# Softplus as one ScalarE activation in a mixer with two MLPs

## The chip, the cores and the metric

The kernel runs on one core of one Trainium2 chip. The metric is the device time of one execution in microseconds (us), the median of several runs. One profiled execution gives the trace; its times are read on the span's own clock, which starts at 0.

## The reference

A state-space mixer over four batches and eight heads gives 3072 tokens of 256 channels. Two MLPs follow, 256 to 2048 to 256. The first one's activation is a softplus, written so that it never overflows; the second one's is a sigmoid approximation of Gelu.

```python
def _moe_ref(x, w_in, w_out):
    h = x @ w_in
    g = np.maximum(h, 0.0) + np.log1p(np.exp(-np.abs(h)))
    return (g @ w_out).astype(np.float32)

def _moe2_ref(x, w_in, w_out):
    h = x @ w_in
    g = h * (1.0 / (1.0 + np.exp(-1.702 * h)))
    return (g @ w_out).astype(np.float32)
```

## The kernel before

The tokens are cut into six chunks (`c`) of 128 positions times four batches, 512 columns each. Each MLP goes through its 2048 hidden channels in 16 slices (`m`) of 128, so that one loop of `2 * NT + 2` = 194 steps `t` runs over both: steps 0 to 95 are the first MLP, 96 to 191 the second. The program's order on each engine is the order of the code (`tc.manual_schedule()`); nothing reorders it.

A step `t` holds, on TensorE, `g1(t)` (six matmuls into the PSUM tile `h`, one of three) and `g2(t - 2)` (the hidden slice times the output weights, accumulated in PSUM `o`). To keep float32 accuracy each operand is a sum of a rounded part and a remainder. `rnd` (ScalarE) makes the rounded part `gh`, `low` (VectorE) the remainder `gl = g - gh`. `g2` takes `wl·gh`, `wh·gh` (L372, L373) and `wh·gl` (L374), for two halves of the output. In the first 16 slices the output weights are not yet split, and `g2` takes two plain float32 matmuls on `g` (L370).

In between, the mixer of the next chunk runs, one sub-chunk in four steps (`k = t % 4`): `cb` matmuls at `k` 0 and 1, their masked products `M` on VectorE (L278), `y` and the state's matmuls at `k` = 2, and at `k` = 3 `xh`/`xl`, the state's update and the long scan `L` (L233) on VectorE. In steps 0 to 13 VectorE also turns the first MLP's float64 weights into float32, one unit a step (`w_sign` L122, `w_join_hi` L127, `w_join_lo` L132); their remainders `w1il` are made on GpSimd. Steps 14 to 29 split the output weights (`w1ol`, VectorE). From step 80 the second MLP's weights are turned, in half units.

The first MLP's softplus is made of four operations on `h`: ScalarE Abs (L546), Exp (L549) and Ln (L561) of the step `t`, and VectorE's `g = max(h, 0) + e` (L542) one step later, at `t + 1`. `rnd(t)` follows on ScalarE at `t + 1`, and `low(t)` on VectorE at the start of step `t + 2`, the step whose `g2(t)` reads it.

Of the kernel before, what the change touches and what calls it, by code (L numbers as in the profile page):

```python
# [9 lines left out]
F32 = mybir.dt.float32  # L10
# [3 lines left out]
AF = mybir.ActivationFunctionType  # L14
ALU = mybir.AluOpType
# [3 lines left out]
T = 128  # L19
# [5 lines left out]
TB = NB * T  # L25
NSUB = NC * NB
NT = NC * NF
# the first chunk's packs have C and B once, its C B^T is taken in plain float32
PL_B, PL_C, PL_X, PL_BN, PL_W = 0, 128, 256, 512, 640
SP_B, SP_C, SP_X, SP_BN, SP_CI, SP_W = 0, 512, 1024, 1280, 1408, 1664  # L30
# 2^-112 turns a float64's exponent, read in the high word as a float32's, into one that float32 holds
HI_SCALE = 2.0**-112


# [1 line left out]
def mixer_two_mlps(ctx: ExitStack, tc: tile.TileContext, pack_p, pack_s, a_l, a_rows, consts, w1i, w1o, w2i, w2o, out):  # L36
# [32 lines left out]
    w1oh = wts.tile([P, NF, DM], F32R, name="w1oh")  # L69
    w1ol = wts.tile([P, NF, DM], F32R, name="w1ol")  # L70
    x2 = wts.tile([P, NC, 2, TB], F32, name="x2")
    # the whole float32 w1o, until the second block splits it
    w1of = x2[:, 2:6].rearrange("p c k t -> p (c k t)").rearrange("p (m f) -> p m f", m=NF)

    def vsub(o, x, y):
# [2 lines left out]
    def psub(o, x, y):  # L78
        nc.gpsimd.tensor_tensor(out=o, in0=x, in1=y, op=ALU.subtract)  # L79

    # a split's two halves, each taken up one step after what it waits for
    act_later, vec_later = [], []

    def split(dst_h, dst_l, src, sub=None):
# [17 lines left out]
        src = w[:, f].rearrange("(k p) f -> p k f", p=P) if kind[-1] == "i" else w[f, :].rearrange("(c p) f -> p c f", p=P)  # L102
        nc.sync.dma_start(out=raw.rearrange("p (a f) -> p a f", a=2), in_=src)

    # float64 bits to float32: the scaled high word holds the exponent and 20 bits of the
    # mantissa three bits too low, the low word the next three
    def w_scale(kind, q, eng):
        if kind[0] == "2" and q in (4, 6):
            # the first block of x2 is out of use by then
            t = x2[:, 0, int(kind == "2o")]  # L110
        else:
            t = stg.tile([P, 512], F32, tag="wt", name=f"wt_{kind}{q}")
        hi = raws[kind, q].bitcast(F32)[:, 1::2]
        if eng is nc.scalar:
            nc.scalar.activation(t, hi, AF.Copy, scale=HI_SCALE)
        else:
            nc.vector.tensor_scalar(out=t, in0=hi, scalar1=HI_SCALE, scalar2=None, op0=ALU.mult)
        return t
# [278 lines left out]

    W1 = (w1ih, w1il)
    with tc.manual_schedule():
        nc.scalar.preload_act_table_set("natural_log_exp_and_others")  # L400
        ac = [hid.tile([P, TB], F32, tag="g", name=f"ac{i}")[0:96, 0 : 2 * T].rearrange("p (k t) -> p k t", k=2) for i in range(3)]
        at_load_p(0)
        nc.sync.dma_start(out=cc, in_=consts)
# [10 lines left out]
        at_spread(0)  # L414
        nc.scalar.activation(eye8[:, TB:].rearrange("p (h t) -> p h t", h=4), eye4, AF.Copy)
        at_scan(0, 0)
        # clipped decays in DRAM, as they are and with the first of each chunk zeroed
        clip(ac[2], ac[0])
        nc.vector.memset(ac[2][:, :, 0:1], 0.0)
        clip(ac[1], ac[0])  # L420
# [86 lines left out]
        for t in range(2 * NT + 2):  # L507
            c, m = divmod(t, NF)
            s, k = (c + 1) * NB + m // 4, m % 4
            mixing = c < NC - 1  # L510
            ended = (t - 2) // NF if t >= 2 and (t - 2) % NF == NF - 1 else None

            if mixing and k in (1, 2) and t != 1:
                at_m(s, k - 1)
            if t < len(W1_units):
                w_sg = w_sign(*W1_units[t])
            if NF <= t - 2 < NT:
                low(t - 2)
            if NT < t <= 2 * NT:
                low(t - 1)  # L520

            if t < NT:
                g1(t, *W1, xh[c], xl[c])
            elif t < 2 * NT:
                g1(t, *w2[0:2], x2h[c - NC], x2l[c - NC])
            if t == 0:
                at_u(NB - 1)
            late = k < 2 or t < NF
            if mixing and not late:
                at_pe(s, k)  # L530
            if 2 <= t < NT + 2:
                g2(t - 2, w1oh, w1ol, plain=w1of if t - 2 < NF else None)
            elif t >= 2:
                g2(t - 2, *w2[2:4])
            if mixing and late:
                at_pe(s, k)

            xl_of = at_out(s) if mixing and k == 3 else None
            if 1 <= t <= NT:
                d = tt[t - 1]  # L540
                d["g"] = hid.tile([P, TB], F32, tag="g", name=f"g{t - 1}")
                nc.vector.scalar_tensor_tensor(out=d["g"], in0=d["h"], scalar=0.0, in1=d["e"], op0=ALU.max, op1=ALU.add)  # L542
            if t < NT:
                d = tt[t]
                e = d["e"] = hid.tile([P, TB], F32, tag="e", name=f"e{t}", bufs=2)
                nc.scalar.activation(e, d["h"], AF.Abs)  # L546
                if t > NF:
                    rnd(t - 1)
                nc.scalar.activation(e, e, AF.Exp, scale=-1.0)  # L549
            elif t < 2 * NT:  # L550
                d = tt[t]
                d["g"] = hid.tile([P, TB], F32, tag="g", name=f"g{t}")
                if t == NT:
                    rnd(t - 1)
                nc.scalar.activation(d["g"], d["h"], AF.Gelu_apprx_sigmoid)  # L555
                rnd(t)
            if ended is not None:
                finish(ended, 0)
                finish(ended, 1)
            if t < NT:  # L560
                nc.scalar.activation(tt[t]["e"], tt[t]["e"], AF.Ln, bias=1.0)  # L561
            if t == 0:
                at_m(s, 0)
            if t < len(W1_units):
                w_join_hi(wt, w_sg)
            catch_up(vec_later)
            catch_up(act_later)

            if t in (1, 3):
                at_state(2 + t // 2)  # L570
            if mixing:
                if k == 0:
                    at_small(s)
                elif k == 1:
                    if s + 1 < NSUB:
                        at_prep(s + 1)
                elif k == 3:
                    xl_of()
                    at_state(s)
                    if s + 1 < NSUB:  # L580
                        at_scan(s + 1)
                    if s + 2 < NSUB:
                        at_load(s + 2)
                    if s == NSUB - 1:
                        at_ctx.close()

            if t < len(W1_units):
                kind, q = W1_units[t]
                if kind == "1o":
                    w_join_lo(kind, q, wt, w1of[:, 2 * q : 2 * q + 2, :].rearrange("p m f -> p (m f)"))  # L590
                else:
                    wi_split(W1, q, w_join_lo(kind, q, wt), psub)
                if t + 1 < len(W1_units):
                    wt = w_scale(*W1_units[t + 1], nc.scalar)
                if t + 3 < len(W1_units):
                    kind, q = W1_units[t + 3]
                    w_load(W_in[kind], kind, q)
            if NF - 2 <= t < 2 * NF - 2 and m % 2 == 0:
                q = (t - NF + 2) // 2
                wo_split((w1oh, w1ol), q, w1of[:, 2 * q : 2 * q + 2, :])  # L600
            if t == (NC - 1) * NF:
                wt2 = ctx.enter_context(tc.tile_pool(name="wt2", bufs=1, reuse_waits="tile"))
                w2 = [
                    wt2.tile(sh, F32R, name=nm)
                    for sh, nm in (([P, 2, DFF], "w2ih"), ([P, 2, DFF], "w2il"), ([P, NF, DM], "w2oh"), ([P, NF, DM], "w2ol"))
                ]
                for kind, q in W2_units[0:3]:
                    w_load(W_in[kind], kind, q)
            # the second layer's weights in half units, the last half of them while it runs
            due = 0  # L610
            if c == NC - 1:
                due = 14 * (m + 1) // 16
            elif c == NC:
                due = min(2 * len(W2_units), 14 + 3 * (m + 1) // 2)
            while halves < due:
                kind, q = W2_units[halves // 2]
                if halves % 2 == 0:
                    half = scaled.pop((kind, q), None) or w_scale(kind, q, nc.vector), w_sign(kind, q)
                else:
                    dst, spl = (w2[0:2], wi_split) if kind == "2i" else (w2[2:4], wo_split)  # L620
                    spl(dst, q, w_join(kind, q, *half), psub)
                    if halves // 2 + 3 < len(W2_units):
                        kind, q = W2_units[halves // 2 + 3]
                        w_load(W_in[kind], kind, q)
                halves += 1
                u = (halves + 1) // 2
                if t >= NT - 1 and u < len(W2_units) and W2_units[u] not in scaled:
                    scaled[W2_units[u]] = w_scale(*W2_units[u], nc.scalar)
            if m == 8 and NC - 1 <= c < 2 * NC - 1:
                x2split(c - NC + 1)  # L630
# [52 lines left out]
```

## Time and profile before

| | |
|---|---|
| time, median of 3 runs (lowest to highest) | 640.23 us (639.79 to 640.71) |
| span of the profiled execution | 638.4 us, 1.8 us below the median |
| TensorE busy with matmuls | 604.7 us, 95% of the span |
| VectorE busy | 430.0 us, 67% |
| ScalarE busy | 397.5 us, 62% |
| GpSimd busy | 154.5 us, 24% |
| chain that ended last | PE 61%, VectorE 26%, issue 5%, ScalarE 4% |

PE is TensorE, PEld its weight loads, DVE VectorE, ACT ScalarE, POOL GpSimd, SPq the DMA-issuing queue. The profiled execution has no separate timing; its own time is its span and what lies around it, and it stands 1.8 us below the median. A matmul's end is modelled and neighbours overlap, so a busy share near 95% does not say how close TensorE is to its best; the starts of the steps say it.

### The profile page before, as it was taken

How to read it: one execution, taken by the hardware profiler on the slowest of the kernel's cores; microseconds unless marked ns; L12 is line 12 of the kernel's file. 1: busy time of each engine (PE TensorE's matmuls, PEld its weight loads, DVE VectorE, ACT ScalarE, POOL GpSimd, SP SyncE). 2: the span in 40 equal slices, each digit the busy share in tenths (PEclk: the TensorE clock that was granted, in tenths of full speed). 3: DMA queues.
4: the chain of work that ended last, by engine and by line, in shares of the span. 5: the costliest groups of instructions: out<-in, count | busy, mean ns of one | idle time of the engine just before them, and what ended most of it. 6: DMA issues, size and time to landing. Idle time of an engine off the chain costs nothing.

```text
span 638.4 us, 8982 instructions
## 1 busy us (share of the span) xinstructions
PE 604.7 (95%) x3392; PEld 455.1 (71%) x3392; DVE 430.0 (67%) x622; ACT 397.5 (62%) x693; POOL 154.5 (24%) x135
## 2 busy tenths in 40 slices
PE   4779889999999999999999999999999999999997
PEld 1345446677677777777777777788888888888886
DVE  5989998999898899989768989723223223232221
ACT  3376666777676767777788887545445445454443
POOL 2555444333434433334102133200000000000000
PEclk8889999999999999999999999999999999999999
DMA  7855644323332332324011224000000000000000
GB/s 225 284 181 198 224 170 144 100 96 119 107 102 95 118 126 95 131 102 153 1 33 67 99 100 131 1 33 2 1 33 1 33 1 1 34 0 1 34 0 33
DMA packets 24411, 54.42 MB, mean 85 GB/s; under 512 B 2832, under 2 KB 8368, under 8 KB 24368
## 3 DMA queue, kind: packets, MB, share of 16 engines
q1 hardware_dynamic: 24368, 53.85, 24.7%
q8 instruction: 26, 0.43, 0.3%
q14 instruction: 17, 0.14, 0.1%
HBM read 50.50 MB, written 3.34 MB: 84 GB/s over the span
## 4 chain that ended last, share of the span: by engine, by line
PE 61%; DVE 26%; issue 5%; ACT 4%; DMA 2%; SPq 1%; POOL 1%; DVEq 0%; ACTq 0%; POOLq 0%
PE h L356 27%; PE o L374 11%; PE o L372 10%; PE o L373 9%; DVE gl L76 6%; DVE L L233 4%; DVE g L542 3%; DVE x L132 1%; DVE wt_2i L127 1%; DVE wt_1o L127 1%; ACT gh L379 1%; DMA wraw_1o<-w1o 1%; PE cb L267 1%; PE y L295 1%; DMA ac<-a_rows 1%
## 5 line engine op out<-in xcount | busy, mean ns | idle before, releaser
L76 DVE TENSOR_TENSOR gl<-g,gh 128x512 fp32r<-128x512 f32 x176 | 152.9, 869 | 162.7 <-ACT gh L379 161.9
L379 ACT ACTIVATE gh<-g 128x512 fp32r<-128x512 f32 x176 | 111.1, 631 | 34.8 <-DVE g L542 31.5
L555 ACT ACTIVATE g<-h 128x512 f32<-128x512 f32 x96 | 57.3, 597 | 113.5 <-PE h L356 113.3
L546 ACT ACTIVATE e<-h 128x512 f32<-128x512 f32 x96 | 57.1, 594 | 39.6 <-PE h L356 39.2
L356 PE MATMUL h<-xh,w1ih 128*128 128x512 f32 x192 | 78.3, 408 | 0.5 <-ACT xh L323 0.5
L374 PE MATMUL o<-gl,w2oh 128*128 128x512 f32 x192 | 75.2, 391 | 0.9 <-DVE gl L76 0.8
L356 PE MATMUL h<-xl,w1ih 128*128 128x512 f32 x192 | 75.8, 395 | 0.0
L372 PE MATMUL o<-gh,w2ol 128*128 128x512 f32 x192 | 74.7, 389 | 0.0
L356 PE MATMUL h<-x2h,w2ih 128*128 128x512 f32 x192 | 74.7, 389 | 0.0
L356 PE MATMUL h<-x2l,w2ih 128*128 128x512 f32 x192 | 74.7, 389 | 0.0
L373 PE MATMUL o<-gh,w2oh 128*128 128x512 f32 x192 | 74.7, 389 | 0.0
L374 PE MATMUL o<-gl,w1oh 128*128 128x512 f32 x160 | 66.0, 412 | 7.7 <-DVE gl L76 7.4
L542 DVE SCALAR_TENSOR_TENSOR g<-h,e 128x512 f32<-128x512 f32 x96 | 65.2, 680 | 4.4 <-ACT e L561 4.2
L372 PE MATMUL o<-gh,w1ol 128*128 128x512 f32 x160 | 64.4, 403 | 0.0
L356 PE MATMUL h<-xh,w1il 128*128 128x512 f32 x192 | 60.3, 395 | 3.9 <-POOL w1il L79 3.9
L373 PE MATMUL o<-gh,w1oh 128*128 128x512 f32 x160 | 62.6, 391 | 0.0
L561 ACT ACTIVATE e<-e 128x512 f32<-128x512 f32 x96 | 60.7, 632 | 2.9
L79 POOL TENSOR_TENSOR rhs_bd<-tc,pk 64x512 fp32r<-64x512 f32 x40 | 61.5, 1539 | 1.5
L549 ACT ACTIVATE e<-e 128x512 f32<-128x512 f32 x96 | 59.5, 620 | 0.5
L356 PE MATMUL h<-x2h,w2il 128*128 128x512 f32 x192 | 59.1, 389 | 0.0
L233 DVE TENSOR_TENSOR_SCAN L<-abz,eye 128x1024 f32<-128x1024 f32 (+1 forms) x25 | 55.9, 2236 | 0.2
L374 PEld LDWEIGHTS o<-gl,w1oh 128*128 128x128 f32 x160 | 30.0, 187 | 25.8 <-DVE gl L76 20.5
(100 smaller groups left out, 896.3 us busy)
## 6 DMA issues: line engine op xcount, KB each, us to landing
pk<-pack_s SPq DMA_DIRECT2D x20, 832.0 KB, 4.5
abz<-scr_z SPq DMA_DIRECT2D x22, 512.0 KB, 3.7
wraw_1i<-w1i SPq DMA_DIRECT2D x8, 512.0 KB, 4.2
wraw_1o<-w1o SPq DMA_DIRECT2D x8, 512.0 KB, 3.3
wraw_2i<-w2i SPq DMA_DIRECT2D x8, 512.0 KB, 3.5
wraw_2o<-w2o SPq DMA_DIRECT2D x8, 512.0 KB, 3.3
out<-ot SPq DMA_DIRECT2D x12, 256.0 KB, 2.2
ad<-scr_a SPq DMA_DIRECT2D x80, 32.0 KB, 2.0
```

The source lines that it names most:

```text
L76: nc.vector.tensor_sub(o, x, y)
L79: nc.gpsimd.tensor_tensor(out=o, in0=x, in1=y, op=ALU.subtract)
L233: nc.vector.tensor_tensor_scan(out=d["L"][:, h].rearrange("p h t -> p (h t)"), data0=d["abz"][:, h].rearrange("p h t -> p (h t)"), data1=e ...
L356: nc.tensor.matmul(h, w[:, k, f], x[:, k, :], start=(n == 0), stop=(n == 5))
L372: nc.tensor.matmul(acc[c][j], wl[:, m, o], d["gh"], start=first, stop=False)
L373: nc.tensor.matmul(acc[c][j], wh[:, m, o], d["gh"], start=False, stop=False)
L374: nc.tensor.matmul(acc[c][j], wh[:, m, o], d["gl"], start=False, stop=last)
L379: nc.scalar.activation(d["gh"], d["g"], AF.Copy)
L542: nc.vector.scalar_tensor_tensor(out=d["g"], in0=d["h"], scalar=0.0, in1=d["e"], op0=ALU.max, op1=ALU.add)
L549: nc.scalar.activation(e, e, AF.Exp, scale=-1.0)
L555: nc.scalar.activation(d["g"], d["h"], AF.Gelu_apprx_sigmoid)
L561: nc.scalar.activation(tt[t]["e"], tt[t]["e"], AF.Ln, bias=1.0)
```

## The change

Softplus becomes one activation that reads `h` in PSUM and writes `g`. Abs, Exp, Ln and the VectorE operation are gone, and with them the tile `e` of the loop. The first MLP's steps get the form of the second's: `g(t)` and, from step 16 on, `gh(t)` are both made in step `t`, and `gl(t)` at the start of step `t + 1`. Another set of ScalarE's tables is loaded at the start.

```diff
-        nc.scalar.preload_act_table_set("natural_log_exp_and_others")
+        nc.scalar.preload_act_table_set("softplus")
...
-            if NF <= t - 2 < NT:
-                low(t - 2)
-            if NT < t <= 2 * NT:
+            if NF < t <= 2 * NT:
                 low(t - 1)
...
-            if 1 <= t <= NT:
-                d = tt[t - 1]
-                d["g"] = hid.tile([P, TB], F32, tag="g", name=f"g{t - 1}")
-                nc.vector.scalar_tensor_tensor(out=d["g"], in0=d["h"], scalar=0.0, in1=d["e"], op0=ALU.max, op1=ALU.add)
-            if t < NT:
-                d = tt[t]
-                e = d["e"] = hid.tile([P, TB], F32, tag="e", name=f"e{t}", bufs=2)
-                nc.scalar.activation(e, d["h"], AF.Abs)
-                if t > NF:
-                    rnd(t - 1)
-                nc.scalar.activation(e, e, AF.Exp, scale=-1.0)
-            elif t < 2 * NT:
+            if t < 2 * NT:
                 d = tt[t]
                 d["g"] = hid.tile([P, TB], F32, tag="g", name=f"g{t}")
-                if t == NT:
-                    rnd(t - 1)
-                nc.scalar.activation(d["g"], d["h"], AF.Gelu_apprx_sigmoid)
-                rnd(t)
+                nc.scalar.activation(d["g"], d["h"], AF.Softplus if t < NT else AF.Gelu_apprx_sigmoid)
+                if t >= NF:
+                    rnd(t)
...
-            if t < NT:
-                nc.scalar.activation(tt[t]["e"], tt[t]["e"], AF.Ln, bias=1.0)
```

The rows of TensorE, GpSimd and the DMA-issuing queue stand in the same order in both programs. Two engines change. The number in `g57` or `gl57` is the step.

VectorE in steps 6 to 8, where it turns weights (`x2` holds the unsplit output weights), before:

```order
L132 SCALAR_TENSOR_TENSOR x2_103<-wraw_1o3_501,wt_1o3_567 128x512
L122 TENSOR_SCALAR wraw_1i5_533<-wraw_1i5_533 128x512
L542 SCALAR_TENSOR_TENSOR g6_632<-h6_574,e6_610 128x512
L127 SCALAR_TENSOR_TENSOR wt_1i5_617<-wt_1i5_617,wraw_1i5_533 128x512
L76 TENSOR_TENSOR xl1_473<-y5_583,xh1_472 128x2x128
L337 SCALAR_TENSOR_TENSOR st1_96<-st1_96,dc5_524,y5_583 128x32 x2
L233 SCALAR_TENSOR_TENSOR L6_643<-abz6_489,eye8_87 128x1024
L132 SCALAR_TENSOR_TENSOR wt_1i5_617<-wraw_1i5_533,wt_1i5_617 128x512
L122 TENSOR_SCALAR wraw_1o4_569<-wraw_1o4_569 128x512
L542 SCALAR_TENSOR_TENSOR g7_672<-h7_622,e7_634 128x512
```

The same place now:

```order
L132 SCALAR_TENSOR_TENSOR x2_103<-wraw_1o3_487,wt_1o3_545 128x512
L122 TENSOR_SCALAR wraw_1i5_515<-wraw_1i5_515 128x512
L127 SCALAR_TENSOR_TENSOR wt_1i5_591<-wt_1i5_591,wraw_1i5_515 128x512
L76 TENSOR_TENSOR xl1_463<-y5_561,xh1_462 128x2x128
L337 SCALAR_TENSOR_TENSOR st1_96<-st1_96,dc5_506,y5_561 128x32 x2
L233 SCALAR_TENSOR_TENSOR L6_613<-abz6_475,eye8_87 128x1024
L132 SCALAR_TENSOR_TENSOR wt_1i5_591<-wraw_1i5_515,wt_1i5_591 128x512
L122 TENSOR_SCALAR wraw_1o4_547<-wraw_1o4_547 128x512
```

One row in each step is gone; the others keep their places.

VectorE from the mixer's sub-chunk 18 to 19 (steps 58 to 60), before:

```order
L76 TENSOR_TENSOR gl56_2597<-g56_2579,gh56_2583 128x512
L542 SCALAR_TENSOR_TENSOR g57_2637<-h57_2563,e57_2581 128x512
L76 TENSOR_TENSOR gl57_2645<-g57_2637,gh57_2641 128x512
L542 SCALAR_TENSOR_TENSOR g58_2661<-h58_2599,e58_2639 128x512
L76 TENSOR_TENSOR xl4_2347<-y18_2606,xh4_2346 128x2x128
L337 SCALAR_TENSOR_TENSOR st2_97<-st2_97,dc18_2553,y18_2606 128x32 x2
L233 SCALAR_TENSOR_TENSOR L19_2672<-abz19_2518,eye8_87 128x1024
L76 TENSOR_TENSOR gl58_2683<-g58_2661,gh58_2665 128x512
L542 SCALAR_TENSOR_TENSOR g59_2701<-h59_2647,e59_2663 128x512
```

And now:

```order
L76 TENSOR_TENSOR gl57_2371<-g57_2357,gh57_2359 128x512
L76 TENSOR_TENSOR gl58_2415<-g58_2411,gh58_2413 128x512
L76 TENSOR_TENSOR xl4_2149<-y18_2380,xh4_2148 128x2x128
L337 SCALAR_TENSOR_TENSOR st2_97<-st2_97,dc18_2331,y18_2380 128x32 x2
L233 SCALAR_TENSOR_TENSOR L19_2438<-abz19_2300,eye8_87 128x1024
L76 TENSOR_TENSOR gl59_2449<-g59_2431,gh59_2433 128x512
```

Ahead of the scan `L19` now stands `gl58`, which stood behind it; each `gl` has moved up by one step.

## Rows read from the trace of the kernel before

**Rows 1.** Windows: us, then each engine's busy us (instructions), granted clock, DMA share, GB/s.

```profile
0.00:44.56 44.56, 27.74 (x218) 13.11 (x218) 35.93 (x53) 21.02 (x43) 21.24 (x25) 0.85 0.72 235
44.56:98.06 53.50, 48.91 (x296) 27.68 (x287) 50.59 (x78) 35.88 (x62) 27.25 (x21) 1.00 0.56 194
98.06:320.61 222.55, 217.50 (x1534) 160.87 (x1533) 199.92 (x289) 159.45 (x284) 83.65 (x73) 1.00 0.30 105
320.61:368.02 47.41, 45.21 (x194) 35.57 (x192) 40.49 (x62) 40.60 (x73) 7.79 (x6) 1.00 0.20 67
368.02:411.59 43.57, 42.17 (x181) 33.32 (x180) 38.56 (x49) 33.02 (x57) 14.60 (x11) 1.00 0.26 85
411.59:638.40 226.81, 223.20 (x985) 184.56 (x983) 64.55 (x95) 107.53 (x178) 0.00 (x0) 1.00 0.04 15
```

**Rows 2.** Waits from 98.06 to 320.61 us: total us, times, longest us.

```profile
PEld o L374 <- DVE gl L76: 15.0, 30, 1.4
...
PE o L374 <- DVE gl L76: 4.7, 7, 1.0
```

**Rows 3.** Page's groups of instructions: busy us, mean ns, then idle us before them.

```profile
L76 DVE TENSOR_TENSOR gl<-g,gh 128x512 fp32r<-128x512 f32 x176 | 152.9, 869 | 162.7 <-ACT gh L379 161.9
L379 ACT ACTIVATE gh<-g 128x512 fp32r<-128x512 f32 x176 | 111.1, 631 | 34.8 <-DVE g L542 31.5
L555 ACT ACTIVATE g<-h 128x512 f32<-128x512 f32 x96 | 57.3, 597 | 113.5 <-PE h L356 113.3
L546 ACT ACTIVATE e<-h 128x512 f32<-128x512 f32 x96 | 57.1, 594 | 39.6 <-PE h L356 39.2
...
L542 DVE SCALAR_TENSOR_TENSOR g<-h,e 128x512 f32<-128x512 f32 x96 | 65.2, 680 | 4.4 <-ACT e L561 4.2
```

**Rows 4.** Timeline of DVE, 48 to 66 us: start us, length us.

```profile
48.42 2.28 DVE L233 TENSOR_TENSOR_SCAN L<-abz,eye 128x1024 f32<-128x1024 f32 x1
...
50.62 0.66 DVE L132 SCALAR_TENSOR_TENSOR wt_1i<-wraw_1i,wt_1i 128x512 uint32<-128x512 uint32 x1
...
51.54 0.68 DVE L542 SCALAR_TENSOR_TENSOR g<-h,e 128x512 f32<-128x512 f32 x1
52.14 0.68 DVE L127 SCALAR_TENSOR_TENSOR wt_1o<-wt_1o,wraw_1o 128x512 uint32<-128x512 uint32 x1
...
60.89 1.67 DVE L132 SCALAR_TENSOR_TENSOR x<-wraw_1o,wt_1o 128x512 uint32<-128x512 uint32 x1
...
65.75 2.28 DVE L233 TENSOR_TENSOR_SCAN L<-abz,eye 128x1024 f32<-128x1024 f32 x1
```

**Rows 5.** Chain that ended last, pieces at step starts: start us, length us.

```profile
98.62 1.39 PE h L356 x6
100.01 1.72 PE o L370 x4
...
246.06 1.37 PE h L356 x6
250.55 1.36 PE h L356 x6
...
297.50 1.39 PE h L356 x6
300.49 1.39 PE h L356 x6
304.87 1.36 PE h L356 x6
307.59 1.36 PE h L356 x6
310.67 1.39 PE h L356 x6
```

**Rows 6.** Timeline of PEld, 254 to 256 us.

```profile
255.11 0.19 PEld L374 LDWEIGHTS o<-gl,w1oh 128*128 128x128 f32 x1 [0.46 <-DVE gl L76]
```

**Rows 7.** Timeline of PE, 38 to 40 us.

```profile
39.07 0.73 PE L356 MATMUL h<-xh,w1il 128*128 128x512 f32 x2 [2.78 <-POOL w1il L79]
```

## The prediction

> **What bounds the kernel now.** I read the starts of the steps first, since with 95% busy nothing can be told from busy time. The first `g1` matmul of step 3 starts at 44.56 us, of step 16 at 98.06, of step 80 at 320.61, of step 96 at 368.02 and of step 111 at 411.59; these cut the windows [rows 1]. Then the chain of waits gives what a step costs when TensorE waits for nothing. In chunk 4 [rows 5] the step with no attention work takes 304.87 to 307.59 = 2.72 us, the steps with `cb` 2.99 and 3.08, the one with `y` 4.38; four steps 297.50 to 310.67 = 13.17. In chunks 1 to 3 the state's matmuls are added to the `y` step, which takes 246.06 to 250.55 = 4.49, so 13.28 for four. In the first chunk the plain `g2` takes 1.72 where the split one takes 2.72 - 1.36 = 1.36, so 4 x 0.36 more: 14.7.
>
> Against these floors:
>
> - Steps 3 to 15: 53.50 us; floor 3 x 14.7 + one step of 1.39 + 1.72 = 47.2. VectorE is busy 50.59 of 53.50 [rows 1]: it is the bound.
> - Steps 16 to 79: 222.55; floor 12 x 13.28 + 4 x 13.17 + 0.7 (steps 16 and 17 still take the plain form) = 212.8. The list of waits names what TensorE waits for: the weight loads of L374 wait 15.0 us for `gl`, the matmuls themselves 4.7 [rows 2]. Loads run ahead of matmuls, so the loss lies between the two; the floor says 9.8. One such wait is in [rows 6].
> - Steps 80 to 95: 47.41; floor 16 x 2.72 = 43.5.
> - Steps 96 to 110: 43.57; floor 15 x 2.72 = 40.8. Only `g2` of steps 94 and 95 is of the old form here.
> - From 411.59 on nothing of the change is left, and VectorE has 64.55 us of work in 226.81. Before 44.56 the first VectorE `g` stands after the work on which TensorE's last long wait hangs, 2.78 us for `w1il` at step 2 [rows 7]; with the granted clock at 0.85 over this stretch I leave it as it is.
>
> **The change, part by part.** *ScalarE.* Abs takes 0.594 us, and it goes with Exp and Ln; one Softplus comes. No row shows Softplus. The nearest rows are the two activations from PSUM of the same 128x512, Abs 594 ns and Gelu 597 ns [rows 3], so I take 0.6 us. No row bounds it from above; what it could cost before it matters is worked out under the last rival. ScalarE waits 39.2 us for `h` before Abs, so time saved there by itself is worth nothing. The Trainium skill, ScalarE: Activation LUTs, What ACT_TABLE_LOAD costs, states 186 ns + 0.833 ns an element whatever the function; by it 512 elements would be an estimated 613 ns and the sum the same. No run here shows it for Softplus, Gelu's 597 agrees.
>
> *VectorE.* 96 operations of 0.68 us go [rows 3]. Neighbours overlap: L542 starts at 51.54 and the next at 52.14 [rows 4], so each frees 0.60.
>
> *Steps 3 to 15.* One sub-chunk is from scan to scan, 48.42 to 65.75 = 17.33 us [rows 4]. Without four L542 it is 17.33 - 2.4 = 14.9, just above TensorE's 14.7. By VectorE: 3 x 14.9 + 3.1 = 47.8, a saving of 5.7; by TensorE's floor 6.3. A lag of 0.2 us per sub-chunk can't reach TensorE within three of them, but `w1il` for the `y` step arrives with little to spare, so I take 5.4. The bounds are 0 (below) and 6.3.
>
> *Steps 16 to 79.* Before, a step's `gl` stood in the same step as the `g2` that reads it, behind the scan (2.28 us) once in four; ScalarE's `gh` itself waited 31.5 us for VectorE's `g` [rows 3]. Now `gh(t)` comes about 0.6 + 0.63 us and two handovers after the end of `g1(t)`: 1.36 + 1.4 = 2.8 us after the step's start, near the start of step t + 1. `gl(t)` follows there (0.9 us on average), and L374 needs it 1.36 + 0.45 us into step t + 2, so 4.5 us after the start of t + 1. The margin is 2.8 us even with an average `gl`; the worst case is `gl` behind the scan, which by my estimate (`xh`, `xl` and the state's update come between) starts 1.5 us into step `k` = 3 and ends 1.1 us into the next, still in time. VectorE's work falls from 199.92 to about 161 (64 x 0.60 less) in 213, 76%. In the new order VectorE stands still behind a `gl` that waits for `gh`, and `M`, `xl` and the scan queue behind it; `M` has some 2 us before `cb` or `y` want it, and TensorE's own 13.28 us a sub-chunk leave that. I take the whole 9.8. Bounds: 0, and 11.1 if the 0.08 us by which the first `cb` step exceeds the second goes as well.
>
> *Steps 80 to 110.* VectorE's 40.49 us fall to 30.9 of about 44, so most of 3.9 goes; I take 3.4 (0 to 3.9), since units of weights come in bursts here. Of the 2.8 lost in steps 96 to 110, 0.6 for the last of the old form (0 to 0.8).
>
> Sum: 5.4 + 9.8 + 3.4 + 0.6 = 19.2, so the span falls from 638.4 to 619.2. The profiled span lies 1.8 us below the median, so the time is 621.0. With every floor reached: 6.3 + 11.1 + 3.9 + 0.8 = 22.1, 618.1.
>
> **The rivals.** *A, the forecast*: all of these stalls go but for small change; 617.5 to 623.5. For it speaks that the floors are taken from steps of this very trace.
>
> *B, the first chunk stays bound by VectorE.* The same operation L132 takes 0.66 us at 50.62 and 1.67 at 60.89 [rows 4]. What is left on VectorE is what stretches, while L542 was 0.68 each time. If the rest slides under GpSimd's work (27.25 us in this stretch) two more of its operations per sub-chunk would take 1 us longer, and of the 5.4 us nothing would be left: 626. For half of that, 624. The Trainium skill, GPSIMD Engine Reference, Specifications, says GpSimd shares its SBUF interfaces with VectorE and collides with its operations of two SBUF inputs or in a two-port mode; L542 reads one input from PSUM, so the trace agrees, with 0.68 against 1.67. Against B: GpSimd's amount of work stays, and the long cases here already meet it.
>
> *C, the new form stalls too.* The second MLP has this form, and where VectorE is loaded (38.56 of 43.57 us) it still loses 2.8 us in 15 steps, 0.19 a step [rows 1]. At that rate 64 steps would lose 12 us and steps 16 to 79 would gain nothing; at half the rate they'd gain 3.7, and the time is 627. Against it: 76% load is not 88%, and from 411.59 on, where VectorE is at 28%, nothing is lost: 81 steps of 2.72 and the two last `g2` of 1.36 are 223 of the 226.81 us, the last copies and the store the rest.
>
> *D, no change.* VectorE is off the path, and TensorE at 95% is the bound. Against it: the floors, and the 15.0 us of waits; it would be 640.
>
> *E, slower.* Softplus is much longer than the other activations. In steps 16 to 79 ScalarE has 222.55 / 64 = 3.48 us a step, and beside Softplus it has `gh` (0.63) and about 0.2 of other work; so it becomes the bound above 2.65 us, 4.4 times Gelu. At 3 us it costs 96 x 0.35 = 34 more, 674. No row shows an activation at such a pace. Were a table loaded at each change between Softplus and the copies, it would be the same case; the program has two loads, as before.
>
> **How the numbers follow.** A has 0.73, B 0.11, C 0.10, D 0.02, E 0.03, and 0.01 is for larger gains. The forecast is A's 621.0. The range must leave out at most 0.2: from 617.5, just under the sum of all floors, through B to the middle of C, 627.5. About 0.2% (1.3 us) is what a measurement of this kernel can tell from no change. A, B and C all end faster by more than that, as do the larger gains: 0.95; D 0.02; E 0.03.
>
> **What would show it.** In the profile after, step 16 should start near 92.7 us, step 80 near 305.4, step 96 near 349, step 111 near 392. From scan to scan in the first chunk 14.7 to 15 us. The waits of L374 for `gl` between steps 16 and 79 fall from 15.0 to under 2 us. Softplus stands at about 0.6 us, and VectorE's idle time before `gl` grows, since it now waits for `gh`. I am wrong in B's way if step 16 starts after 95 with VectorE still at 95%, in C's way if L374 still waits for `gl`, in E's way if Softplus takes over 2.6 us and VectorE's `gl` waits for it in every step.

## The result, and the profile after

The changed kernel takes 622.33 us (median; 621.34 to 622.52), the kernel before 640.16 (639.79 to 640.71): the ratio is 0.9717, with an interval of 0.9704 to 0.9731. The profiled execution's span is 620.5 us, 17.9 below that of before.

The windows of the changed kernel, cut at the same five step starts as [rows 1]: us, then each engine's busy us (PE, PEld, DVE, ACT, POOL), granted clock, DMA share, GB/s.

```profile
0.00:44.66 44.66, 27.91 (x218) 13.74 (x219) 35.78 (x51) 17.71 (x37) 21.89 (x26) 0.89 0.72 235
44.66:96.06 51.40, 48.10 (x295) 27.84 (x287) 48.39 (x65) 21.50 (x38) 26.40 (x21) 1.00 0.61 202
96.06:308.31 212.25, 212.25 (x1534) 163.16 (x1533) 162.37 (x225) 90.47 (x156) 86.36 (x73) 1.00 0.33 110
308.31:351.83 43.52, 43.52 (x193) 36.05 (x192) 31.71 (x47) 24.36 (x42) 8.26 (x6) 1.00 0.23 73
393.23:620.50 227.27, 223.20 (x985) 184.50 (x983) 64.58 (x95) 107.52 (x178) 0.00 (x0) 1.00 0.04 14
```

Steps 96 to 110, the stretch left out, run from 351.83 to 393.23 = 41.40 us. So each stretch gained, in us:

| | start | steps 3-15 | 16-79 | 80-95 | 96-110 | rest | sum |
|---|---|---|---|---|---|---|---|
| predicted | 0 | 5.4 | 9.8 | 3.4 | 0.6 | 0 | 19.2 |
| measured | -0.1 | 2.1 | 10.3 | 3.9 | 2.2 | -0.5 | 17.9 |

In steps 16 to 95 TensorE is busy for the whole window, which it was not before. The first chunk is different: VectorE is still busy 48.39 of 51.40 us, 94%, though an operation of 0.68 us a step has gone.

The page's chain and its groups of the changed kernel; L540 holds Softplus and Gelu together.

```profile
PE 81%; DVE 9%; DMA 4%; issue 3%; SPq 1%; ACT 1%; POOL 0%; DVEq 0%
...
L76 DVE TENSOR_TENSOR gl<-g,gh 128x512 fp32r<-128x512 f32 x176 | 141.7, 807 | 172.6 <-ACT gh L379 172.6
L540 ACT ACTIVATE g<-h 128x512 f32<-128x512 f32 x192 | 114.8, 598 | 256.7 <-PE h L356 253.2
```

Against [rows 3], a Softplus is as long as a Gelu (mean 598 ns, each by itself too). The waits of the changed kernel from 96.06 to 308.31 us (total us, times, longest):

```profile
ACT g L540 <- PE h L356: 112.7, 63, 2.6
...
DVE M L278 <- PE cb L267: 30.3, 26, 2.0
...
DVE gl L76 <- ACT gh L379: 10.1, 17, 1.4
```

The last two in the kernel before, from 98.06 to 320.61 us:

```profile
DVE gl L76 <- ACT gh L379: 10.5, 13, 2.1
...
DVE M L278 <- PE cb L267: 6.3, 16, 1.2
```

The 15.0 and 4.7 us for `gl` of [rows 2] are gone: the other engines now wait for TensorE. VectorE's idle time before `gl`, which was to grow, did not grow in these steps (10.5 and 10.1 us). It grew before `M`, which waits for TensorE's `cb`; before `gl` it grew in steps 80 to 95, from 3.0 to 12.4 us.

### The profile page after: what moved, and what is told of

Read it like the earlier page. It is cut to its first block, busy times and chain, and to the rows that moved or that the text cites. A ratio compares the mean times of both kernels' runs of the same rounds, so it can differ in the third digit from the quotient of the medians.

```text
span 620.5 us, 8790 instructions
## 1 busy us (share of the span) xinstructions
PE 596.1 (96%) x3392; PEld 459.0 (74%) x3392; DVE 378.0 (61%) x526; ACT 293.3 (47%) x501; POOL 157.2 (25%) x135
## 4 chain that ended last, share of the span: by engine, by line
PE 81%; DVE 9%; DMA 4%; issue 3%; SPq 1%; ACT 1%; POOL 0%; DVEq 0%
PE h L356 37%; PE o L372 13%; PE o L374 12%; PE o L373 12%; DMA ad<-scr_a 2%; PE y L295 2%; PE y L289 2%; DVE x L132 1%; PE cb L267 1%; DVE wt_1o L127 1%; DVE L L233 1%; DVE wt_1i L127 1%; DMA ac<-a_rows 1%; PE o L370 1%; DMA wraw_1i<-w1i 1%
## 5 line engine op out<-in xcount | busy, mean ns | idle before, releaser
L76 DVE TENSOR_TENSOR gl<-g,gh 128x512 fp32r<-128x512 f32 x176 | 141.7, 807 | 172.6 <-ACT gh L379 172.6
L540 ACT ACTIVATE g<-h 128x512 f32<-128x512 f32 x192 | 114.8, 598 | 256.7 <-PE h L356 253.2
L79 POOL TENSOR_TENSOR rhs_bd<-tc,pk 64x512 fp32r<-64x512 f32 x40 | 65.1, 1628 | 1.5
L374 PE MATMUL o<-gl,w1oh 128*128 128x512 f32 x160 | 62.4, 390 | 0.0
L233 DVE TENSOR_TENSOR_SCAN L<-abz,eye 128x1024 f32<-128x1024 f32 (+1 forms) x25 | 61.9, 2476 | 0.2
L278 DVE TENSOR_TENSOR M<-cb,L 128x512 f32<-128x512 f32 x48 | 32.7, 686 | 30.5 <-PE cb L267 30.3
L356 PEld LDWEIGHTS h<-xh,w1il 128*128 128x128 f32 x192 | 36.2, 190 | 13.6 <-POOL w1il L79 5.6
L356 PEld LDWEIGHTS h<-xh,w1ih 128*128 128x128 f32 x192 | 36.3, 189 | 8.1 <-ACT xh L323 1.0
L374 PEld LDWEIGHTS o<-gl,w2oh 128*128 128x128 f32 x192 | 36.0, 188 | 8.1 <-DVE gl L76 0.7
L373 PEld LDWEIGHTS o<-gh,w2oh 128*128 128x128 f32 x192 | 36.0, 188 | 7.6
```

The source lines that it names most:

```text
L76: nc.vector.tensor_sub(o, x, y)
L233: nc.vector.tensor_tensor_scan(out=d["L"][:, h].rearrange("p h t -> p (h t)"), data0=d["abz"][:, h].rearrange("p h t -> p (h t)"), data1=e ...
L278: nc.vector.tensor_mul(d["M", g].rearrange("p h t -> p (h t)"), d["cb", g], d["L"][:, 4 * g : 4 * g + 4, :].rearrange("p h t -> p (h t)"))
L356: nc.tensor.matmul(h, w[:, k, f], x[:, k, :], start=(n == 0), stop=(n == 5))
L373: nc.tensor.matmul(acc[c][j], wh[:, m, o], d["gh"], start=False, stop=False)
L374: nc.tensor.matmul(acc[c][j], wh[:, m, o], d["gl"], start=False, stop=last)
```

## The experiments

Starts of steps and lengths of the stretches, us, each read in one trace from the first `g1` matmul of the step. "Scan to scan" is the time between the starts of VectorE's long scans L233, for the first two sub-chunks of the first chunk as in [rows 4]; it hardly hangs on where step 3 starts (e8 and e10 below).

| | step 3 | step 16 | 3-15 | scan to scan | 16-79 | 80-95 | 96-110 | time |
|---|---|---|---|---|---|---|---|---|
| before | 44.56 | 98.06 | 53.50 | 17.33, 17.31 | 222.55 | 47.41 | 43.57 | 640.2 |
| changed | 44.66 | 96.06 | 51.40 | 16.58, 16.58 | 212.25 | 43.52 | 41.40 | 622.3 |
| e9, the changed one again | 45.92 | 97.59 | 51.67 | 18.09, 16.61 | 212.25 | 43.52 | 41.36 | 622.5 |
| e1, old order | 45.58 | 97.09 | 51.51 | 17.38, 17.26 | 213.45 | 44.19 | 41.37 | 624.1 |
| e2, VectorE's operation back | 45.11 | 98.90 | 53.79 | 17.45, 17.46 | 214.08 | 43.52 | 41.37 | 627.9 |
| e5, before without Exp and Ln | 43.43 | 98.89 | 55.46 | 17.44, 17.45 | 222.34 | 44.20 | 42.03 | 635.5 |
| e7, Softplus four times | 42.41 | 95.57 | 53.16 | 16.68, 16.67 | 212.75 | 50.63 | 44.89 | 633.1 |
| e3, `rhs_bd` left out | 44.34 | 91.01 | 46.67 | 15.21, 14.85 | 212.25 | 43.52 | 41.34 | 617.1 |
| e4, `w1il` on VectorE | 45.98 | 95.51 | 49.53 | 16.23, 16.30 | 212.27 | 43.52 | 41.34 | 621.1 |
| e8, less GpSimd work | 42.62 | 94.30 | 51.68 | 16.31, 16.32 | 212.26 | 43.51 | 41.41 | 620.8 |
| e10, e8 again | 45.16 | 94.94 | 49.78 | 16.36, 16.30 | 212.25 | 43.52 | 41.35 | 620.9 |

The runs were on three chips (e1 to e4; e5, e7 and e8; e9 and e10). The kernel before took 640.17, 640.01 and 640.67 us beside them, and each ratio below is against that.

**How well a mark repeats (e9).** The changed kernel itself, without an edit.

> The changed kernel once more, beside the one with less GpSimd work, on one chip. It tells how well the step marks of one profile repeat: step 3 started between 42.4 and 46.0 us in the kernels so far, in which nothing ahead of it differs but the activation. If that is chance of the loads, step 3 starts somewhere in 42 to 46 and step 16, which VectorE's backlog sets, within 1 us of 96.1; steps 16 to 79 take 212.3, 80 to 95 43.5, 96 to 110 41.4, all within 0.2. Total 621 to 623.5 us. The rival, that the marks belong to the kernel: step 3 at 44.7 and steps 3 to 15 in 51.4 us, both within 0.3.

Measured: 622.46 us (ratio 0.9717, 0.9704 to 0.9731); the execution with the profile was its slowest, 623.87. From step 16 on every stretch repeats within 0.05 us. Step 3 started 1.26 us later and step 16 1.53 later, so the two marks move by chance, and step 16 moved a little more than I had expected. What moved step 3 is the granted clock. The end of TensorE's wait at step 2 and the window from 42 to 45 us, first in the changed kernel's first profile and then in e9's:

```profile
39.29 1.22 PE L356 MATMUL h<-xh,w1il 128*128 128x512 f32 x2 [2.77 <-POOL w1il L79]
...
42.00:45.00 3.00, 3.00 (x53) 1.53 (x51) 2.86 (x4) 0.13 (x1) 2.85 (x3) 0.95 0.48 175
```

```profile
39.30 1.22 PE L356 MATMUL h<-xh,w1il 128*128 128x512 f32 x2 [2.78 <-POOL w1il L79]
...
42.00:45.00 3.00, 3.00 (x19) 0.74 (x17) 2.86 (x4) 0.14 (x1) 2.85 (x3) 0.50 0.50 175
```

TensorE had just waited 2.8 us for `w1il` at step 2, in both. In one it was granted 0.95 of 2.4 GHz here and got 53 matmul records done, in the other 0.50 (the lower level) and 19. Step 16 moved for another reason, since VectorE's scan starts at 48.37 us in one and at 48.39 in the other. In e9's first sub-chunk ScalarE's `tb` waits for the transfer of `pk`:

```profile
56.98 0.72 ACT L199 ACTIVATE tb<-pk,cc 128x512 fp32r<-128x512 f32 x1 [2.20 <-DMA pk<-pack_s]
```

GpSimd's `lb` then comes late, and that sub-chunk takes 18.09 us instead of 16.58 (e1 has such a wait there too, of 2.04 us). That the stretch from step 3 to 15 came out nearly the same is chance. It is good to about 2 us in one profile (e8 and e10, one kernel, differ by 1.9), and in the first chunk I read step 16 and the time from scan to scan beside it.

**Which part of the change frees steps 16 to 79 (e1, e2, e5).** e1 keeps the Softplus and puts `rnd` and `low` back where they stood before:

```diff
-            if NF < t <= 2 * NT:
+            if NF <= t - 2 < NT:
+                low(t - 2)
+            if NT < t <= 2 * NT:
                 low(t - 1)
...
+                if t == NT:
+                    rnd(t - 1)
                 nc.scalar.activation(d["g"], d["h"], AF.Softplus if t < NT else AF.Gelu_apprx_sigmoid)
-                if t >= NF:
+                if NF < t < NT:
+                    rnd(t - 1)
+                if t >= NT:
                     rnd(t)
```

> Softplus as one activation, but the rounded part stays one step later and the remainder two steps later, as before. My theory: in steps 16 to 79 both the VectorE work that went and the earlier place of the remainder count, the place the less; VectorE is lighter, but in the first step of each sub-chunk the remainder still stands behind the scan in the very step that reads it, about 0.2 us late, 16 times. So steps 16 to 79 take 215 to 216 us (changed kernel 212.25, before 222.55), the first sixteen steps are as in the changed kernel (step 16 near 96.1), total about 626. Rival (the order alone made the gain): steps 16 to 79 stay at 220 or more. Rival (VectorE's load alone): 212 to 213.

e2 keeps the new order and gives VectorE its operation of 0.68 us back, on a tile that nothing reads:

```diff
+            if 1 <= t <= NT:
+                d = tt[t - 1]
+                e = hid.tile([P, TB], F32, tag="e", name=f"e{t - 1}", bufs=2)
+                nc.vector.scalar_tensor_tensor(out=e, in0=d["h"], scalar=0.0, in1=d["g"], op0=ALU.max, op1=ALU.add)
```

> The changed kernel with the removed VectorE operation put back in its old place, as a max-and-add of the PSUM tile and g into a tile that nobody reads; order of the rest is the new one. My theory (order and load both count, and the operation reads PSUM and so fits beside GpSimd's work in the first chunk): steps 3 to 15 go back from 51.4 to about 53.5 us although 13 x 0.6 = 7.8 us of VectorE work come back; steps 16 to 79 take 213 to 215; total about 625 to 627. Rival (load alone): steps 16 to 79 back to 222, total 638 to 640. Rival (VectorE's time is a plain sum in the first chunk): steps 3 to 15 take 51.4 + 7.8 = 59.

e5 is the kernel before with only ScalarE relieved:

```diff
                 nc.scalar.activation(e, d["h"], AF.Abs)
                 if t > NF:
                     rnd(t - 1)
-                nc.scalar.activation(e, e, AF.Exp, scale=-1.0)
...
-            if t < NT:
-                nc.scalar.activation(tt[t]["e"], tt[t]["e"], AF.Ln, bias=1.0)
```

> The kernel before with Exp and Ln left out (that part of the softplus is not computed): ScalarE is relieved by about as much as in the changed kernel, while VectorE keeps its max-and-add (L542) and the old order stays. My prediction said that ScalarE's time by itself is worth nothing in steps 16 to 79. If so: steps 3 to 15 take 53.5 us (+-0.5) as before, steps 16 to 79 220 to 223, steps 96 to 110 fall from 43.6 to 41.4 if the gain there is ScalarE's, total 634 to 638 us. The rival: e1 (old order) and e2 (VectorE operation kept) have only ScalarE's relief in common, and each has most of the gain, so ScalarE was the cause: steps 16 to 79 take 213 to 216, steps 80 to 95 44 to 45, total 626 to 629.

Measured: 624.12 us (0.9748, 0.9731 to 0.9765), 627.88 (0.9805, 0.9790 to 0.9820) and 635.46 (0.9930, 0.9915 to 0.9945). Steps 16 to 79 in e1, e2 and e5, by windows (of e5 steps 80 to 95 too), and one row of e5's waits in steps 16 to 79:

```profile
97.09:310.54 213.45, 212.94 (x1534) 162.56 (x1533) 163.10 (x225) 82.77 (x155) 85.85 (x73) 1.00 0.33 110
```

```profile
98.90:312.98 214.08, 213.16 (x1535) 162.87 (x1533) 190.60 (x289) 90.49 (x156) 88.47 (x73) 1.00 0.32 109
```

```profile
98.89:321.23 222.34, 217.43 (x1534) 160.96 (x1533) 199.56 (x288) 86.07 (x155) 83.44 (x73) 1.00 0.32 105
321.23:365.43 44.20, 43.83 (x193) 35.96 (x192) 38.31 (x63) 22.70 (x43) 8.22 (x6) 1.00 0.22 72
```

```profile
PEld o L374 <- DVE gl L76: 14.3, 28, 1.4
```

ScalarE's busy time fell from 159 to 86 us in e5, and the stretch gained 0.2: the waits for `gl` are those of [rows 2]. With VectorE's operation gone as well (e1) 9.1 of the 10.3 us come, and with the new order but VectorE still at 190.60 us (e2) 8.5 come. So with ScalarE relieved either is enough for most of it, and they don't add up: the `gl` that came late is mended by less work ahead of it or by a place one step earlier. In e1 the expectation of 215 to 216 was too high; the rival there, the load alone, was nearer. Steps 96 to 110 are 41.37 in both, and e5 has 1.5 of that stretch's 2.2 us and 3.2 of the 3.9 in steps 80 to 95: there ScalarE's relief is most of the gain. The last 0.7 us of steps 80 to 95 are the order's: e1 takes 44.19 without VectorE's operation, e2 43.52 with it. In the first chunk e2 shows what the operation had cost: with all 13 back the stretch is 2.4 us longer, as expected, and not 7.8. e5's 55.46 there is 1.5 above its range, but its step 3 came early; from scan to scan it is as before. e2's total is 0.9 above its range. Whether order or VectorE's relief would do alone with ScalarE as loaded as before was not tried.

**Is the Softplus itself on the path (e7).**

```diff
-                nc.scalar.activation(d["g"], d["h"], AF.Softplus if t < NT else AF.Gelu_apprx_sigmoid)
+                for _ in range(4 if t < NT else 1):
+                    nc.scalar.activation(d["g"], d["h"], AF.Softplus if t < NT else AF.Gelu_apprx_sigmoid)
```

> The changed kernel with the Softplus written four times in each of steps 0 to 95, so ScalarE has 1.8 us more a step and gh is 1.8 us later. By the prediction there is room: gh was to come 2.8 us after the step's start and gl 2.8 us before it is needed, and ScalarE binds above 3.3 us a step in steps 16 to 79. ScalarE then has 4 x 0.6 + 0.63 + 0.2 = 3.2 us a step: steps 3 to 15 unchanged within 1.5 us of 51.4, steps 16 to 79 213 to 217, steps 80 to 95, where a step takes 2.72, bound by ScalarE at 16 x 3.2 = 52 us, total 631 to 636 us. The rival, the Softplus lies on the path that sets the end: 96 x 1.8 = 173 us more, total 795; half hidden, 700.

Measured: 633.08 us (0.9898, 0.9882 to 0.9915). Windows of e7, steps 16 to 79 and 80 to 95:

```profile
95.57:308.32 212.75, 212.57 (x1535) 163.09 (x1533) 147.99 (x225) 198.47 (x348) 81.27 (x73) 1.00 0.33 110
308.32:358.95 50.63, 48.51 (x193) 34.41 (x192) 29.63 (x44) 48.66 (x86) 6.98 (x5) 1.00 0.19 58
```

Steps 16 to 79 lose 0.5 us with 1.8 us more in each step: the margin that the prediction worked out holds this much, and ScalarE at 93% of the window does hardly any harm. In steps 80 to 95, at 2.72 us a step, ScalarE is 96% busy and binds, as rival E would have had it everywhere. The first chunk is as in the changed kernel from scan to scan; the 53.16 us are counted from an early step 3.

**What holds the first chunk (e3, e4, e8, e10).** e3 leaves out `rhs_bd`'s remainders of sub-chunks 5 to 7 (GpSimd); e4 has `w1il` on VectorE in place of GpSimd:

```diff
-        for j in range(2):
+        for j in range(0 if NB < s < 2 * NB else 2):
```

```diff
-                    wi_split(W1, q, w_join_lo(kind, q, wt), psub)
+                    wi_split(W1, q, w_join_lo(kind, q, wt))
```

> The changed kernel without GpSimd's two rhs_bd remainders for sub-chunks 5, 6 and 7 (six operations of 1.53 us; the mixer's values of these sub-chunks are stale, this part of the computation is left out). VectorE's own instructions are the same. My theory (the first chunk stays VectorE-bound because VectorE's operations with two SBUF inputs are stretched beside GpSimd's): L127 and L132 return towards 0.67 us where they were 1.6, a sub-chunk falls from 16.6 to about 15.0 us, steps 3 to 15 from 51.4 to 47.5 to 48.5. Rival (ScalarE's new wait for the w1il buffer, or the ad transfers in front of dc): at most 0.2 us per sub-chunk, 50.8.

> The changed kernel with the remainders w1il of the steps made on VectorE in place of GpSimd: six operations of 1.54 us leave GpSimd in steps 3 to 15, six of about 0.7 come to VectorE, the bound. My theory (GpSimd's work stretches VectorE's by about 0.45 us for each of its own): 9.2 x 0.45 = 4.1 us of stretch go, 6 x 0.65 = 3.9 come, so steps 3 to 15 stay at 51.4 within 1 us. Rival (only VectorE's own list counts): 51.4 + 3.9 = 55.3.

e8 is e4 with those `rhs_bd` on VectorE too, and the start's `cbd` copies on ScalarE; e10 is e8 again beside e9:

```diff
-            psub(
+            (vsub if NB < s < 2 * NB else psub)(
...
-            if g == 1:
-                for h in range(4):
-                    nc.scalar.activation(cbd[:, h * T : h * T + T], d["C"], AF.Identity, scale=mH[:, 4 + h : 5 + h])
-                continue
+            for h in range(4):
+                nc.scalar.activation(cbd[:, h * T : h * T + T], d["C"], AF.Identity, scale=mH[:, 4 * g + h : 4 * g + h + 1])
+            continue
```

> The changed kernel with GpSimd's share of the first chunk cut further: the first MLP's remainders w1il on VectorE (as in e4), those of rhs_bd of sub-chunks 5 to 7 on VectorE too, and the start's cbd copies on ScalarE in place of GpSimd. If GpSimd's work lengthens VectorE's by more than it would take on VectorE itself, steps 3 to 15 fall below e4's 49.5, to 47.2 to 49 us, and the total to 618.5 to 620.5. The rival, only the amount of VectorE's work counts: 3 x about 1.9 us more on VectorE, so steps 3 to 15 take 51 to 53 us, total 622.5 to 625. Step 3 starts at 43 to 46 us as in the other runs if the start is bound by the loads, near 41 if the cbd copies were what it waits for.

> The kernel of e8 once more, on the chip of the changed kernel. If it is really faster, its time is 0.8 to 2 us below the changed kernel's and the intervals of the two ratios part or nearly so; VectorE's L132 and L127 stay at 0.68 to 0.70 us in steps 3 to 15, step 16 starts 1 to 2 us earlier than in the changed kernel. The rival, that the difference was between chips: within 0.5 us of the changed kernel.

Measured: e3 617.14 us (0.9639, 0.9623 to 0.9654), e4 621.13 (0.9702, 0.9686 to 0.9718), e8 620.80 (0.9699, 0.9684 to 0.9713), e10 620.90 (0.9693, 0.9679 to 0.9706). Where GpSimd does less, a sub-chunk is shorter from scan to scan, and most of all in e3; e4's time by itself can't be told from the changed kernel's. The place of [rows 4] in the changed kernel, 48 to 66 us, first GpSimd's timeline, then a row of ScalarE's, and then VectorE's (start us, length us):

```profile
53.04 1.10 POOL L248 TENSOR_TENSOR cd<-dc,pk 128x256 f32<-128x256 f32 x1 [7.35 <-DVE dc L244]
54.10 0.41 POOL L252 TENSOR_TENSOR bs<-pk,L 128x128 f32<-128x128 f32 x1
54.47 1.47 POOL L79 TENSOR_TENSOR w1il<-wt_1i,w1ih 128x512 fp32r<-128x512 f32 x1
55.89 1.73 POOL L79 TENSOR_TENSOR lb<-tb,pk 128x512 fp32r<-128x512 f32 x1
57.58 3.15 POOL L79 TENSOR_TENSOR rhs_bd<-tc,pk 64x512 fp32r<-64x512 f32 x2
60.81 1.60 POOL L79 TENSOR_TENSOR w1il<-wt_1i,w1ih 128x512 fp32r<-128x512 f32 x1
```

```profile
62.44 0.68 ACT L115 ACTIVATE wt_1i<-wraw_1i 128x512 f32<-128x512 f32 x1 [3.61 <-POOL w1il L79]
```

```profile
48.37 2.29 DVE L233 TENSOR_TENSOR_SCAN L<-abz,eye 128x1024 f32<-128x1024 f32 x1
...
51.15 0.42 DVE L122 TENSOR_SCALAR wraw_1o<-wraw_1o 128x512 uint32<-128x512 uint32 x1
...
54.83 1.66 DVE L127 SCALAR_TENSOR_TENSOR wt_1i<-wt_1i,wraw_1i 128x512 uint32<-128x512 uint32 x1
56.52 1.65 DVE L132 SCALAR_TENSOR_TENSOR wt_1i<-wraw_1i,wt_1i 128x512 uint32<-128x512 uint32 x1
58.09 0.68 DVE L278 TENSOR_TENSOR M<-cb,L 128x512 f32<-128x512 f32 x1
58.69 0.90 DVE L122 TENSOR_SCALAR wraw_1o<-wraw_1o 128x512 uint32<-128x512 uint32 x1
59.69 1.59 DVE L127 SCALAR_TENSOR_TENSOR wt_1o<-wt_1o,wraw_1o 128x512 uint32<-128x512 uint32 x1
61.31 1.65 DVE L132 SCALAR_TENSOR_TENSOR x<-wraw_1o,wt_1o 128x512 uint32<-128x512 uint32 x1
63.16 0.43 DVE L122 TENSOR_SCALAR wraw_1i<-wraw_1i 128x512 uint32<-128x512 uint32 x1 [0.20 <-ACT wt_1i L115]
...
64.95 2.29 DVE L233 TENSOR_TENSOR_SCAN L<-abz,eye 128x1024 f32<-128x1024 f32 x1
```

GpSimd's operations end at 55.94, 57.62, 60.73 and 62.41. VectorE's four long ones end at 56.49, 58.17, 61.28 and 62.96: each 0.55 us after, just under the 0.67 that such an operation takes alone. They are not slowed, they wait for the end of the GpSimd operation that they meet. `M`, which reads one input from PSUM, keeps its 0.68 beside `rhs_bd`. The Trainium skill, SBUF — State Buffer, SBUF: two separate sides, says that an operation of VectorE with two SBUF inputs and one of GpSimd that reads SBUF exclude each other for a whole instruction; the trace agrees, with the 0.55 four times.

Before, at the first of these places, the L542 of that step (0.68 us, one input from PSUM) ran beside `w1il`, and the L127 behind it took 1.18:

```profile
54.98 1.48 POOL L79 TENSOR_TENSOR w1il<-wt_1i,w1ih 128x512 fp32r<-128x512 f32 x1
```

```profile
55.22 0.68 DVE L542 SCALAR_TENSOR_TENSOR g<-h,e 128x512 f32<-128x512 f32 x1
55.83 1.18 DVE L127 SCALAR_TENSOR_TENSOR wt_1i<-wt_1i,wraw_1i 128x512 uint32<-128x512 uint32 x1
57.04 0.71 DVE L132 SCALAR_TENSOR_TENSOR wt_1i<-wraw_1i,wt_1i 128x512 uint32<-128x512 uint32 x1
```

Now L127 starts 0.5 us earlier against `w1il` and waits 0.5 longer, and L132, which had come just ahead of GpSimd's `lb`, now meets it (0.71 and 1.65). From scan to scan it is 48.37 to 64.95 = 16.58 us, 0.75 less than in [rows 4] and not the 2.4 of four L542.

VectorE's waits are not the only thing that holds this place. GpSimd works from 53.04 to 62.41 without a pause above 0.1 us; ScalarE's copy `wt_1i`, which has waited 3.61 us for the second `w1il`, ends at 63.12, and VectorE's L122 starts behind it at 63.16, only 0.20 us after L132 was done. So without any wait of its own for GpSimd VectorE would have gained about 0.2 us here: GpSimd's list sets the pace as much as VectorE's. By these rows an L542 that ran while GpSimd was busy cost nothing, and one that ran while it stood still did. In e2 two of the four run beside GpSimd's list and two outside it, and all four together cost 0.87 us from scan to scan. ScalarE's wait for `w1il` (10.8 us, three times, in steps 3 to 15) is new with ScalarE's relief: e5 has it too, the kernel before and e7 don't; why is open.

VectorE's groups in steps 3 to 15 (mean ns behind the busy us), in the kernel before and then in the changed one:

```profile
L127 DVE SCALAR_TENSOR_TENSOR wt_1o<-wt_1o,wraw_1o 128x512 uint32<-128x512 uint32 x6 | 5.5, 924 | 0.0
L127 DVE SCALAR_TENSOR_TENSOR wt_1i<-wt_1i,wraw_1i 128x512 uint32<-128x512 uint32 x5 | 4.4, 876 | 0.0
...
L132 DVE SCALAR_TENSOR_TENSOR wt_1i<-wraw_1i,wt_1i 128x512 uint32<-128x512 uint32 x5 | 3.4, 676 | 0.1
```

```profile
L127 DVE SCALAR_TENSOR_TENSOR wt_1o<-wt_1o,wraw_1o 128x512 uint32<-128x512 uint32 x6 | 6.9, 1153 | 0.3
L127 DVE SCALAR_TENSOR_TENSOR wt_1i<-wt_1i,wraw_1i 128x512 uint32<-128x512 uint32 x5 | 5.4, 1080 | 0.4
L132 DVE SCALAR_TENSOR_TENSOR wt_1i<-wraw_1i,wt_1i 128x512 uint32<-128x512 uint32 x5 | 5.3, 1062 | 0.1
```

The same in e10, with little left to meet on GpSimd:

```profile
L76 DVE TENSOR_TENSOR rhs_bd<-tc,pk 64x512 fp32r<-64x512 f32 x4 | 4.6, 1157 | 0.2 <-ACT tc L199 0.2
L127 DVE SCALAR_TENSOR_TENSOR wt_1o<-wt_1o,wraw_1o 128x512 uint32<-128x512 uint32 x6 | 4.2, 693 | 0.2
...
L76 DVE TENSOR_TENSOR w1il<-wt_1i,w1ih 128x512 fp32r<-128x512 f32 x6 | 4.1, 681 | 0.0
...
L127 DVE SCALAR_TENSOR_TENSOR wt_1i<-wt_1i,wraw_1i 128x512 uint32<-128x512 uint32 x5 | 3.5, 696 | 0.2
L132 DVE SCALAR_TENSOR_TENSOR wt_1i<-wraw_1i,wt_1i 128x512 uint32<-128x512 uint32 x5 | 3.4, 676 | 0.1
```

All are at 0.68 to 0.70 us in e10. But VectorE now carries `w1il` and `rhs_bd`, 8.7 us, and most of what the waits had cost is spent again: from scan to scan e10 takes 16.30 to 16.36 us for the usual 16.6. The time is 1.56 us less than e9's, on the same chip; the two intervals meet only between 0.9704 and 0.9706. Step 16 starts 2.65 us earlier than in e9, but 1.73 of that lies in the sub-chunk in which e9's transfer was late, and 0.63 ahead of the first scan.

In e8 itself step 3 came at 42.62 and steps 3 to 15 took 51.68, the rival's length. Step 3 came early and the stretch is only counted from earlier, for from scan to scan e8 and e10 agree; the total is 0.3 above e8's range. Both theories hold in part: the waits go, and the work that was taken over costs nearly as much. Of the kernels that compute everything, e8 and its repeat e10 have the lowest times; e4's interval overlaps theirs. e4's 49.53 us lie below its expectation of 51.4 within 1, but its step 3 came late, and from scan to scan it gains 0.3.

e3, where the work of `rhs_bd` is left out, comes to 46.67 us, TensorE busy throughout, a little under the floor of 47.2 that the prediction had:

```profile
44.34:91.01 46.67, 46.67 (x297) 28.30 (x287) 43.02 (x65) 21.08 (x37) 18.32 (x16) 1.00 0.65 222
```

VectorE's busy time falls from 48.39 to 43.02 us with the same operations, though the two L127 and the L132 come back only in part (means of 1003, 1072 and 872 ns). e3 and e4 lessen VectorE's waits and GpSimd's list at once. They show that GpSimd's work holds the first chunk, and not how much of it goes by which of the two ways.

## Why the prediction was right, and where its terms were off

The time, 622.3 for 621.0, and the kind of change are as forecast, but the sum was held together by errors of opposite sign: -3.3 in steps 3 to 15, +0.5, +0.5 and +1.6 in the next three stretches, -0.6 in the start and the rest. The largest term, steps 16 to 79, was right by its mechanism; that the total came within 1.3 us is in part luck.

- *Steps 3 to 15* is the mis-sized term: 2.1 for 5.4 us (step 16 at 97.59 in e9 makes it no larger). The step that failed is that each L542 frees 0.60 us of VectorE here, so that VectorE's list alone sets the sub-chunk down to 14.9 us, and the argument against rival B that the long cases already meet GpSimd's work. Two of the four L542 of a sub-chunk had run beside GpSimd's list, and the time that they leave goes to waits for GpSimd. In the sums over the stretch the 13 operations were 8.7 us (each frees 0.60, so 7.8), and the two L127 and the L132 together grew from 13.3 to 17.6 us. That leaves 3.5 for the 2.1 measured; the other 1.4 us are not put down to rows. From scan to scan it came to 16.58 us, where GpSimd's list and ScalarE's copy behind it end within 0.2 us of VectorE's. Mark B, step 16 after 95 us with VectorE near 95% busy, came true at 96.06 and 94% (97.59 and 89% in e9). B took somewhat more than half of the term, and e3 shows that GpSimd's work is behind it.
- *Steps 16 to 79*: 10.3 for 9.8, the stretch is 212.25 against a floor of 212.8. Rival C is out: the new form does not stall when VectorE has 76% to do, and in e2, with VectorE at 89% (190.60 of 214.08 us), the stretch is only 1.8 us longer, where C's rate would have cost 12. The prediction named the two causes, the place of `gl` and VectorE's work, and took them as one; e1 and e2 show that either does for most. That ScalarE's time alone is worth nothing here holds (e5), and the margin held 1.8 us more of Softplus (e7). The margin of 2.8 us was added up wrongly, though nothing hangs on it: with `gl` from about 0.1 to 1.0 us and needed at 4.5, its own terms give 3.5.
- *Steps 80 to 95*: the floor of 43.5 was reached, 3.9 for 3.4. The reason given was VectorE's relief; e5 gives 3.2 of it with VectorE's work nearly as it was (38.31 us busy for 40.49), and so it was mostly ScalarE, busy 40.60 of 47.41 us before [rows 1].
- *Steps 96 to 110*: 2.2 for 0.6. I had counted only the last two `g2` of the old form. e5 gains 1.5 us here, and e7, with ScalarE loaded in the steps ahead, loses 3.5 against the changed kernel: ScalarE's load in the first MLP's last steps reaches into the second's first ones. So most of what rival C took for a stall of the new form there was none. That it does so by the weight units that it leaves behind is argued, not shown.
- *Rivals D and E* are out: Softplus takes what Gelu takes, and e7 shows where a longer one begins to bind, in steps 80 to 95.

## What to carry to other kernels

Before counting the time that a removed VectorE operation frees, see what stands beside it on GpSimd: an operation with a PSUM input may have been filling time in which the two-input ones have to wait anyway, or in which GpSimd's own list sets the pace. Busy time does not tell: an operation that waits for GpSimd is a long one in the profile. Compare a stretch with its floor engine by engine, and ask of each relief alone what it gives, since two reliefs of one late tile don't add. And where a stretch is bound by VectorE and GpSimd together, moving work from one to the other gave little here (0.3 us a sub-chunk), and only leaving it out (e3) shortened it much.

## What the runs showed of the hardware

A VectorE operation on two SBUF tiles of 128x512 (L127, L132) takes 0.67 to 0.70 us alone and ends 0.55 us after the GpSimd operation that it met, up to 1.66 us long, four times of four in the rows above; one with an input from PSUM (`M`, L542) takes 0.68 us either way. L122, which reads one SBUF tile, took 0.42 us at 51.15 and 0.90 beside `rhs_bd`. TensorE's granted clock in the first 46 us was not the same in two profiles of one kernel, 0.95 and 0.50 from 42 to 45 us, behind the same wait of 2.8 us. Softplus of 128x512 from PSUM costs ScalarE 0.6 us, as Gelu does.
